# Scores of two pairs in one operation, five attention banks and three layer banks, and other assumed times in a planned kernel

## The chip, the cores and the metric

The kernel runs on one core of a Trainium2 chip. Five engines work side by side, each through its own instructions in order: PE (TensorE, the matrix products), DVE (VectorE), ACT (ScalarE), POOL (GpSimd) and SP (SyncE, which here issues every DMA). Matrix products write to PSUM, which has eight banks; DVE and ACT read them out to SBUF. The metric is the time of one execution on the device in microseconds, the median of several runs; less is better.

## The reference

Two attentions are computed from q, k, v of shape (8, 8, 576, 64) and added, and the sum goes through two dense layers with a maximum of three products:

```python
q_d, k_d, v_d = (a.reshape(B, H, S // 4, 4, D).mean(axis=3) for a in (q, k, v))
out_up = np.repeat(sm_attn(q_d, k_d, v_d), 4, axis=2)        # pooled attention
mask = np.abs(pos[:, None] - pos[None, :]) < 4               # seven neighbours
out_local = softmax(np.where(mask, scale * q @ k.T, -1e9)) @ v
x = (out_up + out_local).transpose(0, 2, 1, 3).reshape(4608, 512)
h = np.maximum(np.maximum(x @ w1, x @ w2), x @ w3)           # 512 -> 768
return h @ w_out                                             # 768 -> 512
```

All of it is float32. (The lines are shortened; `sm_attn` is a softmax attention with the scale 1/8.)

## The kernel before

**Tiling.** The 4608 tokens are cut into nine blocks of 512: block j < 8 is the first 512 tokens of batch j, and block 8 holds the last 64 tokens of all eight batches. The attention of a block has two groups, n = 2j and 2j+1, each of four heads in two pairs (`pr` = 0, 1); so the groups run from 0 to 17. The layers of a block (`mlp_in`, `mlp_out`) follow its attention.

**Layers.** Operands are split into a high and a low float32r part, and three products stand for one. `mlp_in(j)` has 6 x 3 accumulations of 12 matmuls of 128x512; ACT or DVE reads each bank out (into `t`, with the maximum), then ACT and DVE split the result into `hh`. `mlp_out(j)` has 4 accumulations of 18 matmuls, read by ACT into `y` and stored. That is 288 layer matmuls per block. Each layer bank is a tile of the tag `pm`.

**Attention.** For a group from 4 on: `load_qk` loads a q and k tile per pair (three buffers); `window_scores` computes a pair's scores against 70 neighbours for each 64 queries, 16 float32 products into two banks of the tag `pa` (a float32 product shows as two passes in the profile, 32 in all); `scores` copies them to `sm`, stores them to a scratch in DRAM with two DMAs per pair, and loads back the seven diagonals as `s` for the softmax. `values` multiplies and adds `v` on ACT, POOL and DVE. Beside it `pooled_scores` makes the pooled attention with three `pa` banks, stores the transposed probabilities to DRAM in eight DMAs (`pdd`) and loads them as `pt` (one DMA) and `ptt` (two); `pooled_values` multiplies them with the pooled v into one `pa` bank, read by ACT as `od`. Then `transposes` adds `od` to x and splits the sum into `xhi` and `xlo`. The groups 0 to 3 (`DENSE`) do the neighbours by a banded product instead (`band_scores`, `band_values`); block 0 takes its banks for that from `pm`, block 1 from `pa`.

**Order.** No instruction is issued when its line runs. A `Recorder` collects all operations, and `place` makes a list schedule of them on assumed costs: of the operations that are ready on an engine it takes the first, by priority, and an operation that opens a tile waits until its buffers are free. The buffers of a tag are given out in the order in which tiles were recorded. `emit` then issues everything in the planned order from line 415, which is why every row of the profile shows L415. On the chip each engine runs its own list in order; where an input is later than assumed, the engine waits and all behind it too.

PE operations of the attention have a priority 2000 ahead of their group's, so they go before layer matmuls as soon as the plan has them ready. The layers have priority -100, `transposes` -200, group n has 100n, and the weights have 60 to 350. `together()` makes several PE calls one operation that nothing else is put between, with 200 ns for the turn (`RUN_NS`).

Margins in the plan: `lag` (600 ns) is added between an operation and a user on another engine, `pelag` in its place where the user is on PE, `dlag` is the least that is added behind a DMA, and the costs of all engines but PE are multiplied by `SLOW`. The line that applies them:

```python
u.ready = max(u.ready, free[e] if same else o.end + max(u.lag, u.dlag if e == "SP" else 0.0))
```

A DMA is assumed to take 530 ns of SP (times the factor) and to land 1200 ns plus its bytes plus 1100 ns later. Layers, `transposes` and the groups 0 to 3 have neither `dlag` nor factor. The order of the `pa` banks around a group: three of `pooled_scores(n)`, two and two of the scores of group n+1 (`begin(n + 1)` is recorded there), one of `pooled_values(n)`, three of `pooled_scores(n + 1)`.

Of the kernel before, what the change touches and what calls it, by code (L numbers as in the profile page):

```python
# [10 lines left out]
F32 = mybir.dt.float32  # L11
# [5 lines left out]
PSUM = bass.MemoryType.PSUM  # L17
# [3 lines left out]
P = 128  # L21
NO = 7
FAC = 4
# [8 lines left out]
XBUFS = 5  # L32
VBUFS = 3
LAG = 600.0
PELAG = 2500.0
DMA_LAG = 2000.0
SLOW = 1.15
SEG = FAC * P
QT = 64
KWIN = QT + NO - 1  # L40
# [4 lines left out]
DENSE = tuple(range(2 * BANDED))  # L45
# [71 lines left out]
class Recorder:  # L117
# [6 lines left out]
    def __init__(self, nc, tc, sb, psum, dr):  # L124
        self.nc, self.tc, self.pools = nc, tc, {"SB": sb, "PSUM": psum, "DRAM": dr}
        self.names = bacc.Bacc("TRN2", target_bir_lowering=False, num_devices=1)
        self.ops, self.tags, self.of, self.masks = [], {}, {}, {}
        self.prio, self.lag, self.pelag, self.run = 0.0, 0.0, 0.0, None
        self.engines = {"PE": nc.tensor, "DVE": nc.vector, "ACT": nc.scalar, "POOL": nc.gpsimd, "SP": nc.sync}

    def tile(self, shape, dtype, tag=None, bufs=1, name=None, space="SB"):
# [32 lines left out]
    def add(self, forms, bias={}):  # L164

        o = Op()
        o.forms, o.bias = forms, bias
        outs, ins = [], []
        for method, args, kw in next(iter(forms.values())):
            named = [k for k in ("out", "accum_out") if is_ap(kw.get(k))]  # L170
            w = [kw[k] for k in named]
            r = [a for a in args if is_ap(a)] + [v for k, v in kw.items() if is_ap(v) and k not in named]
            if "out" not in named:
                w.append(args[0])
                r = r[1:]
            outs += w
            ins += r
        o.prio = self.prio
        if "PE" in forms and o.prio >= 0.0:
            o.prio -= 2000.0  # L180
        o.dlag = 0.0 if self.pelag == self.lag else DMA_LAG
        o.lag = self.lag if "PE" not in forms else self.pelag
        o.seq = len(self.ops)
        o.need, o.tiles = set(), []
        pe = "PE" in forms
        for write, aps in ((False, ins), (True, outs)):
            for ap in aps:
                r = self.region(ap)
                if r is None:
                    continue  # L190
                info, p0, p1, m = r
                bufs, order = self.tags[info["tag"]]
                assert info["k"] == 0 or info["k"] + bufs >= len(order), ("used after its buffer was given on", info["name"])
                for q, w, a0, a1, am, was_pe in info["acc"]:
                    if (w or write) and q is not o and (info["psum"] or (a0 < p1 and p0 < a1 and (am & m))) and not (w and write and info["tag"][0] == "DRAM"):
                        o.need.add(q)
                if not info["ops"] or info["ops"][-1] is not o:
                    info["ops"].append(o)
                    o.tiles.append(info)
                if write and info["psum"] and pe:  # L200
                    info["acc"] = [x for x in info["acc"] if not (x[1] and x[5])]
                info["acc"].append((o, write, p0, p1, m, pe))
        self.ops.append(o)
        return o
# [37 lines left out]
    def place(self):  # L242
        ops = self.ops
        for o in ops:
            o.users, o.left, o.ready, o.eng, o.waits = [], len(o.need), 0.0, None, []
            o.cost = {}
            for e, calls in o.forms.items():
                c = [self.price(e, *x) for x in calls]
                turn = RUN_NS if e == "PE" and len(calls) > 1 else 0.0
                o.cost[e] = ((sum(x[0] for x in c) + turn) * (1.0 if e == "PE" or not o.dlag else SLOW), any(x[1] for x in c))  # L250
        for o in ops:
            for q in o.need:
                q.users.append(o)
# [179 lines left out]
def local_global_attention_maxout_kernel(ctx: ExitStack, tc: tile.TileContext, qk_d, qke_d, vw_d, wi_d, wo_d, v, ident_d, mask_d, diag_d, band_d, out):  # L433
# [8 lines left out]
        return rec.tile(shape, dtype, tag, bufs, name)  # L442

    def bank(shape, tag, name):
        return rec.tile(shape, F32, tag, {"pm": 4, "pa": 4}[tag], name, "PSUM")

    @contextmanager
    def at(prio, lag=0.0, pelag=None):
        was = rec.prio, rec.lag, rec.pelag
        rec.prio, rec.lag, rec.pelag = prio, lag, lag if pelag is None else pelag  # L450
        yield
        rec.prio, rec.lag, rec.pelag = was

    @contextmanager
    def together():
# [34 lines left out]
    state = {}  # L490
# [183 lines left out]
        act.mul(odtail[:, c, j], po[:, :, P:], 0.25)  # L674


    def window_scores(n, pr, tag="pa"):
        step = QT if n // 2 < B else KWIN
        qk = state[n]["qk"][pr]
        sps = [bank([P, FAC, KWIN], tag, f"sb_{n}_{pr}_{i}") for i in range(2)]  # L680
        with together():
            for t in range(SEG // QT):
                u, h = divmod(t, 2)
                for i in range(2):
                    pp = slice(64 * i, 64 * i + 64)
                    pe.matmul(sps[i][QT * h : QT * h + QT, u], qk[pp, 0, 3 + QT * t : 3 + QT * t + QT], qk[pp, 1, step * t : step * t + KWIN], start=True, stop=True, tile_position=(64 * i, QT * h))
        return sps

    def scores(n):
        j = n // 2  # L690
        st = state[n]
        scr = rec.tile([SCR], F32, "scr", 2, f"scr_{n}", "DRAM")
        for pr in range(2):
            sps = window_scores(n, pr)
            sm = new([P, 2, FAC, KWIN], tag="sm", bufs=2, name=f"sm_{n}_{pr}")
            for i in range(2):
                copy(sm[:, i], sps[i])
            for h in range(2):
                to = (2 * pr * SEG + h * QT) * (KWIN + 1)
                sp.dma_start(dram(scr, to, [[KWIN, QT], [P * (KWIN + 1), 2 * FAC], [1, KWIN]]), sm[QT * h : QT * h + QT].rearrange("p g u x -> p (g u) x"))  # L700
        s = st["p"] = new([P, FAC, HH, NO], tag="s", bufs=2, name=f"s_{n}")
        sp.dma_start(s, dram(scr, 0, [[FAC * (KWIN + 1), P], [KWIN + 1, FAC], [SEG * (KWIN + 1), HH], [1, NO]]))
        e0 = 0 if j < B else FAC
        sf = s[..., e0 : e0 + 3]
        dve.tensor_tensor(out=sf, in0=sf, in1=mask[:, j // B].unsqueeze(2).broadcast_to([P, FAC, HH, 3]), op=ALU.min)
        mx = new([P, FAC, HH], tag="mx", bufs=2, name=f"mx_{n}")
        dve.tensor_reduce(out=mx, in_=s, axis=AX.X, op=ALU.max)
        dve.tensor_tensor(out=s, in0=s, in1=mx.unsqueeze(3).broadcast_to([P, FAC, HH, NO]), op=ALU.subtract)
        act.activation(s, s, AF.Exp, scale=0.125)
        z = new([P, FAC, HH], tag="z", bufs=2, name=f"z_{n}")  # L710
        dve.tensor_reduce(out=z, in_=s, axis=AX.X, op=ALU.add)
        dve.tensor_scalar_add(z, z, EPS)
        dve.reciprocal(z, z)
        dve.tensor_tensor(out=s, in0=s, in1=z.unsqueeze(3).broadcast_to([P, FAC, HH, NO]), op=ALU.mult)
# [42 lines left out]
            vw[g] = t  # L757

    def band_scores(n, pr, tag):
        sps = window_scores(n, pr, tag)  # L760
        sm = new([P, 2, FAC, KWIN], tag="sm", bufs=2, name=f"sm_{n}_{pr}")
        for i in range(2):
            dve.tensor_tensor(out=sm[:, i], in0=sps[i], in1=bandmask, op=ALU.min)
        mx = new([P, 2, FAC], tag="mxb", bufs=2, name=f"mxb_{n}_{pr}")
        z = new([P, 2, FAC], tag="zb", bufs=2, name=f"zb_{n}_{pr}")
        dve.tensor_reduce(out=mx, in_=sm, axis=AX.X, op=ALU.max)
        dve.tensor_scalar_mul(mx, mx, -0.125)
        for i in range(2):
            for u in range(FAC):
                act.activation(sm[:, i, u], sm[:, i, u], AF.Exp, bias=mx[:, i, u : u + 1], scale=0.125, accum_out=z[:, i, u : u + 1])  # L770
        dve.tensor_scalar_add(z, z, EPS)
        dve.reciprocal(z, z)
        muls = [("mul", (sm[:, i, u], sm[:, i, u], z[:, i, u : u + 1]), {}) for i in range(2) for u in range(FAC)]
        one = [("tensor_tensor", (), dict(out=sm, in0=sm, in1=z.unsqueeze(3).broadcast_to([P, 2, FAC, KWIN]), op=ALU.mult))]
        rec.add({"DVE": one, "POOL": one, "ACT": muls})
        state[n]["sm", pr] = sm
# [114 lines left out]
    def attention(n):  # L891
# [21 lines left out]
            tail_pooled(n)  # L913
            pooled_scores(n)
        if n < 2 * B + 1:
            with at(100.0 * n + 100.0, LAG, PELAG):
                begin(n + 1)
        values(n)
        if j < B:
# [1 line left out]

    def block(j):
        for n in (2 * j, 2 * j + 1):
            with at(100.0 * n, LAG, LAG if n in DENSE else PELAG):
                attention(n)
        if DENSE and 2 * j + 1 == DENSE[-1]:
            with at(100.0 * n + 100.0, LAG, PELAG):
                begin(n + 1)

    def turn(j):  # L930
# [49 lines left out]
```

## Time and profile before

| what | value |
|---|---|
| median of 3 runs | 736.38 us (734.8 to 737.51) |
| the profiled execution | 741.36 us, its span 739.5 us |
| DMA | 100.28 MB, mean 136 GB/s |
| DVE busy, 20 to 140 us | 111.8 of 120 us |

The profile is one execution. A busy PE row is not a rate: a 128x512 matmul shows 0.39 us but the next starts after 0.23, so starts are counted. In a row of the stretches stand the stretch, its length, then busy time and (in brackets) instructions of PE, PE's weight loads, DVE, ACT and POOL, then the granted clock of PE, the DMA share and GB/s. In a row of the timeline stand the start, the duration, the engine, the operation, the tile written and the tiles read, the shape, the count, and in square brackets the idle time before it and what ended that. In PE's list of waits stand the total, the count and the longest. Buffer numbers are left out of names, and a name such as `t` or `wo` is a buffer that several tiles share.

### The profile page before, as it was taken

Reading aid. Unit: us, or ns where it says so; the run is one execution under the profiler, and the core shown is the slowest. Engines: PE = TensorE matmul, PEld = TensorE weight load, DVE = VectorE, ACT = ScalarE, POOL = GpSimd, SP = SyncE. Lnnn points to the kernel's source line nnn. Section 1 sums busy time; section 2 is a strip of 40 time slices with the busy share of each in tenths; the row PEclk is TensorE's granted clock in tenths of the full one; section 3 lists DMA queues with packets and bytes.
Section 4 is the critical chain, followed back from the end, with each engine's and each line's share of the span. In section 5 each row is a group of like instructions: output and inputs, shape, how many; then the busy total and the mean of one; then the engine's idle time right before and its main releaser. Section 6 shows DMA issues by size and latency. Waiting matters only on the chain.

```text
span 739.5 us, 13101 instructions
## 1 busy us (share of the span) xinstructions
PE 698.1 (94%) x4544; PEld 559.7 (76%) x4544; DVE 523.3 (71%) x1002; ACT 396.3 (54%) x1359; POOL 175.0 (24%) x265
## 2 busy tenths in 40 slices
PE   3749999999999999999998999999989999999997
PEld 2637777778787787878686878787867888888885
DVE  6899999847978887878886869788775677331220
ACT  4685565447748284846656456477572675121111
POOL 0002000005524251543523133134151332000000
PEclk9959999999999999999999999999999999999999
DMA  8945321676585677847675746585866551120002
GB/s 285 364 133 194 119 98 58 184 169 148 134 175 143 160 163 177 182 97 149 175 151 148 160 126 136 160 161 139 151 189 120 104 150 34 26 71 29 1 0 58
DMA packets 189599, 100.28 MB, mean 136 GB/s; under 512 B 161262, under 2 KB 165389, under 8 KB 188765
## 3 DMA queue, kind: packets, MB, share of 16 engines
q1 hardware_dynamic: 189533, 99.44, 53.6%
q8 instruction: 36, 0.59, 0.3%
q14 instruction: 30, 0.25, 0.1%
HBM read 70.18 MB, written 29.23 MB: 134 GB/s over the span
## 4 chain that ended last, share of the span: by engine, by line
PE 72%; DVE 11%; DMA 10%; SPq 3%; issue 2%; ACT 2%; DVEq 0%; ACTq 0%
PE pm L415 65%; PE pa L415 6%; SPq L415 3%; DMA traw<-in_v_dram 3%; DVE pvb L415 2%; DMA qk<-in_qk_dram 2%; DVE wo L415 2%; DVE t L415 2%; DMA ptt<-pdd 1%; DVE sm L415 1%; DMA out_dram<-y 1%; DMA x<-in_vw_dram 1%; DMA pt<-pdd 1%; ACT pvb L415 1%; DMA pvb<-in_wo_dram 1%
## 5 line engine op out<-in xcount | busy, mean ns | idle before, releaser
L415 PE MATMUL pm<-xlo_0r,whi_0r 128*128 128x512 f32 x648 | 254.8, 393 | 0.0
L415 PE MATMUL pm<-xhi_0r,wlo_0r 128*128 128x512 f32 x648 | 253.8, 392 | 0.0
L415 PE MATMUL pm<-xhi_0r,whi_0r 128*128 128x512 f32 x648 | 253.4, 393 | 0.0
L415 POOL TENSOR_TENSOR pvb<-v,s 128x256 f32<-128x256 f32 x209 | 147.0, 734 | 192.8 <-DVE s L415 61.7
L415 ACT ACTIVATE pvb<-v,s 128x64 f32<-128x64 f32 x732 | 184.7, 340 | 9.7 <-DVE s L415 5.1
L415 DVE TENSOR_TENSOR t<-pm,t 128x512 f32<-128x512 f32 x108 | 74.2, 687 | 99.3 <-PE pm L415 95.3
L415 PEld LDWEIGHTS pm<-xhi_0r,whi_0r 128*128 128x128 f32 x648 | 121.9, 188 | 26.4 <-issue 1.1
L415 PEld LDWEIGHTS pm<-xlo_0r,whi_0r 128*128 128x128 f32 x648 | 121.8, 188 | 26.4 <-issue 0.9
L415 PEld LDWEIGHTS pm<-xhi_0r,wlo_0r 128*128 128x128 f32 x648 | 121.9, 188 | 25.6 <-issue 0.6
L415 DVE TENSOR_TENSOR pvb<-pvb 128x768 f32<-128x768 f32 x112 | 99.0, 884 | 10.9 <-POOL pvb L415 8.7
L415 ACT CAST hh_0r<-t 128x512 fp32r<-128x512 f32 x54 | 33.5, 621 | 133.9 <-DVE t L415 133.6
L415 PE MATMUL pm<-wo_1r,hh_0r 128*128 128x512 f32 x216 | 85.2, 395 | 0.0
L415 PE MATMUL pm<-wo_0r,hh_1r 128*128 128x512 f32 x216 | 84.8, 394 | 0.0
L415 PE MATMUL pm<-wo_0r,hh_0r 128*128 128x512 f32 x216 | 83.2, 393 | 1.4 <-ACT wo_0r L415 0.9
L415 ACT COPY t<-pm 128x512 f32<-128x512 f32 x54 | 31.6, 585 | 40.4 <-PE pm L415 40.3
L415 ACT COPY y<-pm 128x512 f32<-128x512 f32 (+1 forms) x44 | 25.4, 583 | 50.3 <-PE pm L415 40.9
L415 PEld LDWEIGHTS pm<-wo_0r,hh_0r 128*128 128x128 f32 x216 | 40.4, 188 | 10.9 <-ACT wo_0r L415 1.8
L415 PEld LDWEIGHTS pm<-wo_1r,hh_0r 128*128 128x128 f32 x216 | 40.6, 188 | 9.7 <-DVE wo_1r L415 0.8
L415 PEld LDWEIGHTS pm<-wo_0r,hh_1r 128*128 128x128 f32 x216 | 40.5, 188 | 8.7 <-issue 0.4
L415 DVE TENSOR_TENSOR hh_1r<-t,hh_0r 128x512 fp32r<-128x512 f32 x54 | 38.7, 717 | 9.9 <-ACT hh_0r L415 9.6
L415 ACT CAST xhi_0r<-t 128x512 fp32r<-128x512 f32 x32 | 19.5, 617 | 16.7 <-DVE t L415 12.6
L415 PEld LDWEIGHTS pa<-qk 64*64 64x64 f32 x1024 | 18.9, 133 | 12.1 <-issue 4.4
(119 smaller groups left out, 706.6 us busy)
## 6 DMA issues: line engine op xcount, KB each, us to landing
qk<-in_qk_dram SPq DMA_DIRECT2D x32, 582.0 KB
v<-in_v_dram SPq DMA_DIRECT2D x55, 320.0 KB
out_dram<-y SPq DMA_DIRECT2D x36, 256.0 KB
scr<-sm SPq DMA_DIRECT2D x56, 140.0 KB
xd<-x SPq DMA_DIRECT2D x112, 64.0 KB
t<-xd SPq DMA_DIRECT2D x28, 256.0 KB
wo<-in_wi_dram SPq DMA_DIRECT2D x4, 1536.0 KB
pdd<-pd SPq DMA_DIRECT2D x48, 80.0 KB
```

Source lines behind the costliest of these rows:

```text
L415: getattr(self.engines[o.eng], method)(*map(real, args), **{k: real(x) for k, x in kw.items()})
```

## The change

Four things at once.

- `window_scores` takes a list of pairs and puts the products of all of them into one `together()`. `scores` calls it for both pairs, so one PE operation opens four `pa` banks and makes 32 products; the copies and DMAs follow per pair as before. `band_scores` calls it with one pair.
- The PSUM banks are divided anew: `pa` has five instead of four, `pm` three instead of four.
- `PELAG`, `DMA_LAG` and `SLOW` give way to a triple by group: below group 8 `pelag` 2000, `dlag` 1500, factor 1.1; from group 8 on 3000, 3000, 1.2. Before, it was 2500, 2000, 1.15 for all groups from 4 on.
- Groups 0 to 3 have no triple (`None`): then `pelag` is `lag`, `dlag` 0 and the factor 1, as before.

```diff
-PELAG = 2500.0
-DMA_LAG = 2000.0
-SLOW = 1.15
+CARE = {"near": (2000.0, 1500.0, 1.1), "far": (3000.0, 3000.0, 1.2)}
+NEAR = 8
...
-        o.dlag = 0.0 if self.pelag == self.lag else DMA_LAG
-        o.lag = self.lag if "PE" not in forms else self.pelag
+        pelag, o.dlag, o.slow = self.care or (self.lag, 0.0, 1.0)
+        o.lag = pelag if "PE" in forms else self.lag
...
-                o.cost[e] = ((sum(x[0] for x in c) + turn) * (1.0 if e == "PE" or not o.dlag else SLOW), any(x[1] for x in c))
+                o.cost[e] = ((sum(x[0] for x in c) + turn) * (1.0 if e == "PE" else o.slow), any(x[1] for x in c))
...
-        return rec.tile(shape, F32, tag, {"pm": 4, "pa": 4}[tag], name, "PSUM")
+        return rec.tile(shape, F32, tag, {"pm": 3, "pa": 5}[tag], name, "PSUM")
...
+    def care(n):
+        return None if n in DENSE else CARE["near" if n < NEAR else "far"]
...
-    def window_scores(n, pr, tag="pa"):
+    def window_scores(n, prs, tag="pa"):
         step = QT if n // 2 < B else KWIN
-        qk = state[n]["qk"][pr]
-        sps = [bank([P, FAC, KWIN], tag, f"sb_{n}_{pr}_{i}") for i in range(2)]
+        sps = {pr: [bank([P, FAC, KWIN], tag, f"sb_{n}_{pr}_{i}") for i in range(2)] for pr in prs}
         with together():
-            for t in range(SEG // QT):
+            for pr in prs:
+                qk = state[n]["qk"][pr]
+                for t in range(SEG // QT):
...
+        both = window_scores(n, range(2))
         for pr in range(2):
-            sps = window_scores(n, pr)
+            sps = both[pr]
...
-            with at(100.0 * n + 100.0, LAG, PELAG):
+            with at(100.0 * n + 100.0, LAG, care(n + 1)):
                 begin(n + 1)
...
-            with at(100.0 * n, LAG, LAG if n in DENSE else PELAG):
+            with at(100.0 * n, LAG, care(n)):
                 attention(n)
```

More of the change, by code (lines that the diff above doesn't have):

```diff
@@ L127, in __init__ @@
         self.ops, self.tags, self.of, self.masks = [], {}, {}, {}
-        self.prio, self.lag, self.pelag, self.run = 0.0, 0.0, 0.0, None
+        self.prio, self.lag, self.care, self.run = 0.0, 0.0, None, None
         self.engines = {"PE": nc.tensor, "DVE": nc.vector, "ACT": nc.scalar, "POOL": nc.gpsimd, "SP": nc.sync}
@@ L444, in bank, with at @@
     def bank(shape, tag, name):
-        return rec.tile(shape, F32, tag, {"pm": 4, "pa": 4}[tag], name, "PSUM")
+        return rec.tile(shape, F32, tag, {"pm": 3, "pa": 5}[tag], name, "PSUM")
     @contextmanager
-    def at(prio, lag=0.0, pelag=None):
-        was = rec.prio, rec.lag, rec.pelag
-        rec.prio, rec.lag, rec.pelag = prio, lag, lag if pelag is None else pelag
+    def at(prio, lag=0.0, care=None):
+        was = rec.prio, rec.lag, rec.care
+        rec.prio, rec.lag, rec.care = prio, lag, care
         yield
-        rec.prio, rec.lag, rec.pelag = was
+        rec.prio, rec.lag, rec.care = was
+    def care(n):
+        return None if n in DENSE else CARE["near" if n < NEAR else "far"]
     @contextmanager
@@ L674, in pooled_values @@
         act.mul(odtail[:, c, j], po[:, :, P:], 0.25)
-    def window_scores(n, pr, tag="pa"):
+    def window_scores(n, prs, tag="pa"):
         step = QT if n // 2 < B else KWIN
-        qk = state[n]["qk"][pr]
-        sps = [bank([P, FAC, KWIN], tag, f"sb_{n}_{pr}_{i}") for i in range(2)]
+        sps = {pr: [bank([P, FAC, KWIN], tag, f"sb_{n}_{pr}_{i}") for i in range(2)] for pr in prs}
         with together():
-            for t in range(SEG // QT):
[L683 to L686, printed above, removed]
+            for pr in prs:
+                qk = state[n]["qk"][pr]
+                for t in range(SEG // QT):
+                    u, h = divmod(t, 2)
+                    for i in range(2):
+                        pp = slice(64 * i, 64 * i + 64)
+                        pe.matmul(sps[pr][i][QT * h : QT * h + QT, u], qk[pp, 0, 3 + QT * t : 3 + QT * t + QT], qk[pp, 1, step * t : step * t + KWIN], start=True, stop=True, tile_position=(64 * i, QT * h))
         return sps
@@ L759, in band_scores @@
     def band_scores(n, pr, tag):
-        sps = window_scores(n, pr, tag)
+        sps = window_scores(n, (pr,), tag)[pr]
         sm = new([P, 2, FAC, KWIN], tag="sm", bufs=2, name=f"sm_{n}_{pr}")
@@ L923, in block @@
         for n in (2 * j, 2 * j + 1):
-            with at(100.0 * n, LAG, LAG if n in DENSE else PELAG):
+            with at(100.0 * n, LAG, care(n)):
                 attention(n)
         if DENSE and 2 * j + 1 == DENSE[-1]:
-            with at(100.0 * n + 100.0, LAG, PELAG):
+            with at(100.0 * n + 100.0, LAG, care(n + 1)):
                 begin(n + 1)
```

## The prediction

> **What bounds the kernel now.** I read the page's busy rows and slices first, then busy time by stretch, the groups of matmuls, the chain of waits and PE's own list of waits.
>
> ```profile
> span 739.5 us, 13101 instructions
> PE 698.1 (94%) x4544; PEld 559.7 (76%) x4544; DVE 523.3 (71%) x1002; ACT 396.3 (54%) x1359; POOL 175.0 (24%) x265
> PE   3749999999999999999998999999989999999997
> PEclk9959999999999999999999999999999999999999
> ```
>
> PE is busy from the fourth slice to the last, at full clock but for the third slice. The stretches price a layer matmul, and the groups count them:
>
> ```profile
> 55.00:149.00 94.00, 92.24 (x771) 71.36 (x771) 86.59 (x157) 52.41 (x155) 7.45 (x11) 1.00 0.42 132
> ...
> 603.00:717.00 114.00, 114.00 (x505) 94.48 (x504) 39.62 (x61) 31.56 (x84) 10.03 (x15) 1.00 0.13 34
> ```
>
> ```profile
> L415 PE MATMUL pm<-xhi_0r,whi_0r 128*128 128x512 f32 x648 | 253.4, 393 | 0.0
> ...
> L415 PE MATMUL pm<-wo_0r,hh_0r 128*128 128x512 f32 x216 | 83.2, 393 | 1.4 <-ACT wo_0r L415 0.9 <-ACT hh_0r L415 0.5
> ```
>
> From 603 to 717 us 505 layer matmuls start in 114.00 us, with nothing between them: 0.226 us each. There are three groups of 648 and three of 216, 2592 in all, so 585 us of the span is layer work that the change leaves as it is. The first of them starts here:
>
> ```profile
> 54.66 0.69 PE L415 MATMUL pm<-xhi_0r,whi_0r 128*128 128x512 f32 x1
> ```
>
> 54.7 + 585 is 639.4 us. The other 100 us is attention on PE, the turns between the two kinds of work, PE's stalls and the last store. The chain of waits ends in 158 us of layer work alone:
>
> ```profile
> 576.03 158.01 PE pm L415 x696
> ```
>
> So the attention is finished that long before the end, and from 55 us on only what PE itself spends or waits counts. A change there is worth its PE time; before 55 us, DVE and the loads count.
>
> **Part 1: two score operations become one.** A pair's scores are a run of 32 passes between layer matmuls:
>
> ```profile
> 194.13 0.39 PE L415 MATMUL pm<-xhi_0r,whi_0r 128*128 128x512 f32 x1
> 194.45 0.72 PE L415 MATMUL pa<-qk 64*64 64x70 f32 x32
> 195.09 0.51 PE L415 MATMUL pm<-xlo_0r,whi_0r 128*128 128x512 f32 x1
> 195.43 0.40 PE L415 MATMUL pm<-xhi_0r,wlo_0r 128*128 128x512 f32 x1
> ```
>
> From 194.13 to 195.43 is 1.30 us and holds two layer steps, 0.45 us; the run costs 0.85 us. Its passes take 195.09 - 194.45 = 0.64 us, so entering and leaving cost 0.21 us. The merged run is 64 passes and one turn, so each of the 14 groups 4 to 17 saves one turn: **-2.9 us**. Groups 2 and 3 still go pair by pair. No instruction is added; the copies and the four stores to the scratch follow as before. The added wait: all four banks must be free before the first pass, and behind it on PE stand the layer matmuls. With five banks, two are free beside the three of the pooled scores, so two of those must have been read by ACT's exponentials, where today's second pair needs all three. PE's list of waits (below) has no wait on a qk load, so the second pair's load hides as it does now; uncovered, it would cost its landing.
>
> **Part 2: assumed times.** These move no instruction's own cost, only its place in the order. PE's waits after 140 us:
>
> ```profile
> PE pa L415 <- DMA pt<-pdd: 3.2, 3, 1.8
> PE pa L415 <- DMA ptt<-pdd: 2.0, 2, 1.8
> PE pa L415 <- ACT pd L415: 0.8, 1, 0.8
> PE pa L415 <- ACT pdt L415: 0.6, 1, 0.6
> PE pm L415 <- ACT hh_0r L415: 0.5, 1, 0.5
> ```
>
> 5.2 us is waiting for the pooled probabilities to come back from DRAM. The largest case beside a clean one, in PE's timeline:
>
> ```profile
> 389.88 0.39 PE L415 MATMUL pm<-xlo_0r,whi_0r 128*128 128x512 f32 x1
> 390.79 0.47 PE L415 MATMUL pa<-pt,vd 128*64 128x144 f32 x4 [0.52 <-DMA pt<-pdd]
> 393.09 0.75 PE L415 MATMUL pa<-ptt,vtail 128*64 128x144 f32 x4 [1.83 <-DMA ptt<-pdd]
> ...
> 394.73 1.33 PE L415 MATMUL pa<-qkT 64*128 64x144 f32 x8
> ...
> 396.55 0.50 PE L415 MATMUL pm<-xhi_0r,wlo_0r 128*128 128x512 f32 x1
> ...
> 434.69 0.39 PE L415 MATMUL pm<-wo_0r,hh_0r 128*128 128x512 f32 x1
> ...
> 437.20 0.50 PE L415 MATMUL pm<-wo_1r,hh_0r 128*128 128x512 f32 x1
> ```
>
> The same work takes 396.55 - 389.88 = 6.67 us at group 10 and 437.20 - 434.69 = 2.51 us at group 11. Of the 4.2 us excess 2.35 is idle; the other 1.8 is slow matmuls, since the clock drops:
>
> ```profile
> 380.00:400.00 20.00, 17.65 (x89) 13.68 (x88) 12.01 (x28) 6.76 (x24) 7.25 (x13) 0.91 0.67 169
> ```
>
> 9% of 20 us is the same 1.8 us. The Trainium skill ("TensorE: Matmul & The Clock Gate", "What's actually happening") says that the clock falls to half after about one idle window of 3.4 us that runs freely; the trace agrees in the drop, though 2.35 us idle was enough here. By it a shorter stall would lose the slow matmuls whole, and the sum would stay as it is below.
>
> The other waits of late groups:
>
> ```profile
> 538.64 0.47 PE L415 MATMUL pa<-pt,vd 128*64 128x144 f32 x4 [1.78 <-DMA pt<-pdd]
> 539.26 0.47 PE L415 MATMUL pa<-ptt,vtail 128*64 128x144 f32 x4 [0.15 <-DMA ptt<-pdd]
> ...
> 572.41 0.47 PE L415 MATMUL pa<-pt,vd 128*64 128x144 f32 x4 [0.91 <-DMA pt<-pdd]
> ```
>
> Group 14 idles 1.9 us, with 1.8 us of slow matmuls as at group 10, 3.7; group 15 0.9; a score run waiting for ACT 0.8. With 4.2 that makes 9.6 us. For groups from 8 on the plan adds 3000 - 2500 = 500 ns before PE may use a landed load, 3000 - 2000 = 1000 ns between the stores and that load, and 1.2 for 1.15 on each cost. An SP issue is then assumed at 530 x 1.2 = 636 ns, was 610; the row says 650:
>
> ```profile
> L415 SPq DMA_DIRECT2D ptt<-pdd x24: 610/650/692, 166.7 to 567.8; - x24
> ```
>
> Eleven issues make 0.3 us, so PE's turn comes about 1.8 us later. Taken from idle times of 2.35, 1.93, 0.91 and 0.8 that leaves 0.6 us, so up to 9.0 us is recovered; nothing, if later turns are met by equally later loads. I take two thirds, **-6.0 us**, since three of eight late groups waited and the two big ones are cured by the delay alone. PE has layer matmuls to fill it; nothing is late next, with 158 us in hand.
>
> Groups 4 to 7 get 500 ns less at each of the two hops and 1.1 for 1.15. The plan assumes about 2.4 us of landing (1200 + 1100 ns and the bytes); with 2.0 us of margin that is 4.4 us. Two late loads took:
>
> ```profile
> 387.90 5.15 DMA ptt<-pdd
> ...
> 534.95 4.18 DMA ptt<-pdd
> ```
>
> By the one an early group would wait 0.75 us, by the other nothing. For groups 5, 6, 7 that is 0 to 2.3 us; **+0.5 us**, nearer nothing, because none of them waits today.
>
> **Part 3: one layer bank less.** An accumulation is 12 matmuls (2.7 us) in a layer's first half, 18 (4.1 us) in its second. In the steady state the bank given up costs nothing while ACT or DVE reads a bank within two accumulations, 5.4 us. It counts where PE runs ahead into several banks because an input is late. Two such places, with the input that comes last and the pm matmuls issued before it:
>
> ```profile
> 221.00:233.90 12.90, 9.62 (x40) 1.00 0.60 168
> 120.80:143.40 22.60, 14.80 (x54) 1.00 0.53 157
> ```
>
> ```profile
> 233.23 0.68 DVE L415 TENSOR_TENSOR xlo_0r<-t,xhi_0r 128x512 fp32r<-128x512 f32 x1
> ...
> 142.79 0.65 ACT L415 CAST wo_0r<-pvb 128x512 fp32r<-128x512 f32 x1 [0.46 <-DVE pvb L415]
> ```
>
> At the start of layer 2 the fourth xlo is there at 233.9. Three banks hold 3 x 11 = 33 matmuls that do without it; 40 were issued, so 7 x 0.226 = 1.6 us has no bank. In layer 0's second half the last output weight is there at 143.4; three banks hold 3 x 15 = 45, 54 were issued: 2.0 us. Below, the plan fills both with other work (0); above, the whole bank, 2.7 and 4.1 us. I take **+3.6 us**, the count of the rows.
>
> The start has it too: block 0's band work uses the layer banks.
>
> ```profile
> 25.74 1.21 PE L415 MATMUL pm<-qk 64*64 64x70 f32 x32
> ...
> 31.23 0.69 DVE L415 TENSOR_TENSOR t<-pm,od 128x512 f32<-128x512 f32 x1 [0.81 <-ACT od L415]
> ```
>
> ```profile
> 35.67 0.73 DVE L415 TENSOR_REDUCE mxb<-sm 128x8 f32<-128x560 f32 x1
> ```
>
> Group 1's first scores at 25.74 take two banks while two value banks wait to be read from 31.23 on. With three they must wait till 31.9, six us later, but the first reduction is at 35.67, so most of it hides; DVE's copies move. Bounds -1 (five attention banks loosen block 1) and +3 (half of the six); I take **+0.5**.
>
> **Sum:** -2.9 - 6.0 + 0.5 + 3.6 + 0.5 = -4.3 us on the profiled 741.36 us (span 739.5 and 1.9 around it), 737.1. The median shown, 736.38, lies 5.0 lower; the same difference gives **732.1 us**, 0.6% faster.
>
> **The rivals.** What a measurement can tell from no change is 0.5%, 3.7 us: below 732.7 and above 740.1.
>
> *The late stalls move, they don't go.* The loads follow ACT, DVE and SP, all replanned. For it: five of the eight late groups met their loads without a wait under the old margin, so lateness depends on the order. Against: the two large waits are short of the added 1.8 us by 0.6 at most. Without part 2's gain: -2.9 + 0.5 + 3.6 + 0.5 = +1.7, **738.1 us**.
>
> *Three banks starve the layers: slower.* Place: the first accumulations of layers 1 to 3 and layer 0's second half, where x or weights come just in time. Price: a bank's worth each, 3 x 2.7 + 4.1 = 12.2 us, with half of part 2: -2.9 - 3.0 + 0.5 + 12.2 + 0.5 = +7.3, **743.7 us**. For it: 55 to 149 us has DVE busy for 86.59 of 94 us, so a late reader can't catch up. Against: from 603 to 717 us no bank waits at all. It decides once bank waits exceed 2.9 + 6.0 + 3.7 - 1.0 = 11.6 us.
>
> *Bank waits that also drop the clock.* Each could cost the 1.8 us of the 0.91 row; once in each of nine layers is 16.2 us, -4.3 + 16.2 = +11.9, **748.3 us**. The slices show no drop with four banks except beside DMA stalls. The Trainium skill (the same page, "A second HAM failure mode: psum-queue depth-cycling") tells of such a kernel, whose PE idled between groups as it cycled through banks; no run here shows it yet.
>
> *Everything lands:* -2.9 - 9.0 and nothing given back, -11.9, **724.5 us**.
>
> **Chances.** The forecast 0.48, everything landing 0.08; the moved stalls 0.24; starved banks 0.17, with the clock 0.03. The forecast's own range (728 to 736) lies partly inside 0.5%: I leave 0.42 of its 0.48 on the faster side, so faster 0.50, same 0.30, slower 0.20. Range 724.5 to 742: it leaves out the clock case, half of the starved banks and the best end of "everything".
>
> **What would show it.** Score runs of x64 with one turn (about 1.5 us between layer matmuls), 14 of them. PE's waits on pt and ptt near 1 us instead of 5.2, and a granted clock of 1.00 from 60 us on. PE waiting for ACT t, DVE t or ACT y ahead of pm matmuls near 120 to 150 and 220 to 235 us would be the bank's price. The first layer matmul at 54 to 58 us. The forecast is wrong if layer 0's second half ends more than 4 us later than before, or if pt waits return at other groups.

## The result and the profile after

| | before | changed |
|---|---|---|
| median | 736.4 us (734.8 to 737.51, 6 runs) | 729.13 us (727.95 to 733.91, 6 runs) |
| ratio, 95% | | 0.9915 (0.9886 to 0.9944) |
| profiled execution, its span | 741.36, 739.5 us | 728.81, 726.4 us |
| first layer matmul | 54.66 us | 55.51 us |

The ratio takes 0.85% off, 6.3 us, and the medians lie 7.3 us apart; 4.3 us were forecast. The page of the changed kernel begins as follows (span, busy time of each engine, then two rows in 40 slices):

```profile
span 726.4 us, 13076 instructions
PE 688.0 (95%) x4544; PEld 555.2 (76%) x4544; DVE 520.1 (72%) x993; ACT 399.4 (55%) x1365; POOL 177.1 (24%) x268
PE   2739999999999999999999999999999999999996
PEclk9959999999999999999999999999999999999999
```

The two 8s that PE's row had in its second half are 9s now, and PE has as many matmuls as before. The stretches of the changed kernel (columns as before, the granted clock third from the end) say the same from 60 us on, the last row being pure layer work:

```profile
60.00:380.00 320.00, 317.20 (x2236) 253.76 (x2237) 262.37 (x511) 196.33 (x683) 88.50 (x133) 1.00 0.62 152
380.00:580.00 200.00, 199.48 (x1324) 161.26 (x1323) 150.68 (x288) 115.14 (x412) 65.94 (x97) 1.00 0.65 145
603.00:717.00 114.00, 114.00 (x505) 94.39 (x504) 43.71 (x68) 34.96 (x101) 11.43 (x17) 1.00 0.17 41
```

In its last 200 us of attention PE lacks 0.5 us, and the 505 layer matmuls still start in 114.00 us. PE's list of waits of the changed kernel, 140 to 720 us, is complete here:

```profile
PE pa L414 <- DMA ptt<-pdd: 0.6, 1, 0.6
PE pm L414 <- DVE hh_1r L414: 0.5, 1, 0.5
PE pm L414 <- DVE xlo_0r L414: 0.4, 1, 0.4
PE pm L414 <- ACT hh_0r L414: 0.2, 1, 0.2
```

The 5.2 us of waiting for `pt` and `ptt` are 0.6. In PE's timeline of the changed kernel, here are a score run with its neighbours and group 10's pooled values, which took 6.67 us before:

```profile
187.31 0.39 PE L414 MATMUL pm<-xhi_0r,wlo_0r 128*128 128x512 f32 x1
187.62 1.21 PE L414 MATMUL pa<-qk 64*64 64x70 f32 x64
188.76 0.50 PE L414 MATMUL pm<-xhi_0r,whi_0r 128*128 128x512 f32 x1
189.10 0.40 PE L414 MATMUL pm<-xlo_0r,whi_0r 128*128 128x512 f32 x1
...
392.14 0.39 PE L414 MATMUL pm<-xhi_0r,whi_0r 128*128 128x512 f32 x1
392.46 0.47 PE L414 MATMUL pa<-pt,vd 128*64 128x144 f32 x4
...
394.65 0.50 PE L414 MATMUL pm<-xlo_0r,whi_0r 128*128 128x512 f32 x1
```

From 187.31 to 189.10 is 1.79 us with two layer steps, 0.45 us, in it: the merged run costs 1.34 us where two runs cost 2 x 0.85. That is 0.36 us less a group, and there are 14 such runs in the trace, the first at 133.71 and the last at 577.60. Group 10's passage takes 394.65 - 392.14 = 2.51 us, as a clean one.

**A measure that leaves the start out.** Each layer has 288 layer matmuls, so the 289th begins layer 1 and the 2017th layer 7. In the changed kernel they are these two rows of PE's timeline:

```profile
150.42 0.40 PE L414 MATMUL pm<-xhi_0r,whi_0r 128*128 128x512 f32 x1
...
590.24 0.39 PE L414 MATMUL pm<-xhi_0r,whi_0r 128*128 128x512 f32 x1
```

From one to the other is 439.82 us. This stretch holds all attention groups but the first few. The table has it for every kernel that was profiled, beside the sum of PE's list of waits from 155 to 600 us and the time lost to a granted clock under 1 (that of each 10 us from 155 to 605, its lack times 10 us, added up). The kernels after the second row are told in the next section; each row is one execution.

| kernel | layer 1 starts | 1 to 7 | waits | lost to clock |
|---|---|---|---|---|
| before, first profile | 148.88 | 454.43 | 6.5 | 3.4 |
| changed | 150.42 | 439.82 | 1.7 | 0 |
| e1 before again | 150.00 | 447.60 | 3.3 | 0 |
| e2 merge only | 148.12 | 461.35 | 13.7 | 8.5 |
| e3 times only | 147.74 | 451.60 | 4.9 | 1.7 |
| e4 banks only | 154.33 | 442.07 | 0.2 | 0 |
| e5 merge and banks | 148.52 | 447.64 | 8.0 | 0 |
| e6 banks and times | 153.66 | 442.04 | 0.6 | 0 |
| e7 late groups old | 153.93 | 449.99 | 8.0 | 1.7 |
| e8 early groups old | 149.15 | 439.69 | 2.6 | 0 |
| e9 three and four banks | 155.60 | 446.87 | 3.8 | 0 |
| e10 late margins alone | 154.66 | 442.17 | 3.6 | 0 |
| e11 late factor alone | 150.03 | 451.54 | 8.8 | 1.7 |
| e12 all groups late | 156.50 | 445.75 | 5.7 | 3.5 |

Where "1 to 7" is long, PE waits or runs at a lower clock. With the last two columns taken off, 437 to 441 us are left in the kernels with merged scores and 441 to 445 in the others. The measure has a spread of its own: the kernel before, whose PE order is the same in both rows, has 454.43 and 447.60. So a difference of a few us between two rows is a sign, and the ratios of the next section decide.

### The profile page after: what moved, and what is told of

It is laid out like the page before. It is cut to its first block, busy times and chain, and to the rows that moved or that the text cites. A ratio compares the mean times of both kernels' runs of the same rounds, so it can differ in the third digit from the quotient of the medians.

```text
span 726.4 us, 13076 instructions
## 1 busy us (share of the span) xinstructions
PE 688.0 (95%) x4544; PEld 555.2 (76%) x4544; DVE 520.1 (72%) x993; ACT 399.4 (55%) x1365; POOL 177.1 (24%) x268
## 4 chain that ended last, share of the span: by engine, by line
PE 59%; DVE 2%; DMA 2%; SPq 1%; POOL 0%; issue 0%; ACT 0%; DVEq 0%; ACTq 0%
PE pm L414 55%; PE pa L414 4%; SPq L414 1%; DMA t<-xd 1%; DVE pvb L414 1%; DMA pdd<-pd 0%; DMA ptt<-pdd 0%; POOL pvb L414 0%; DVE t L414 0%; DVE hh_1r L414 0%; DVE x L414 0%; DVE pd L414 0%; DVE xlo_0r L414 0%; ACT y L414 0%; DVE sm L414 0%
## 5 line engine op out<-in xcount | busy, mean ns | idle before, releaser
L414 ACT ACTIVATE pvb<-v,s 128x64 f32<-128x64 f32 x728 | 182.0, 339 | 12.3 <-DVE s L414 7.7
L414 DVE TENSOR_TENSOR pvb<-pvb 128x768 f32<-128x768 f32 x112 | 100.5, 897 | 8.0 <-ACT pvb L414 3.8
L414 POOL TENSOR_TENSOR hv<-v 128x128 f32<-128x128 f32 (+1 forms) x19 | 14.1, 745 | 74.5 <-DMA v<-in_v_dram 55.7
```

What stands on the lines that cost most here:

```text
L414: getattr(self.engines[o.eng], method)(*map(real, args), **{k: real(x) for k, x in kw.items()})
```

## The experiments

All kernels compute everything. e1 to e4 ran beside the kernel before at 735.88 us, e5 to e8 beside 736.3, e9 to e12 beside 734.9 (medians of 23, 35 and 27 runs). Two experiments of different calls are compared by their ratios to it.

**e1, the kernel before once more.** No edit.

> The kernel before, unchanged, profiled once more. If the two long waits of PE for the pooled probabilities (groups 10 and 14 in the first profile, 4.2 and 3.7 us with their slow matmuls) belong to the planned order, they return at the same two groups, and the profiled time lies near 741 us. If they are an accident of that one execution, other groups wait, or none does, and the profiled time lies near the median of 736 us.

Measured: 735.57 us, span 733.8. In its timeline, the pooled values of groups 10 and 14:

```profile
390.69 0.47 PE L415 MATMUL pa<-pt,vd 128*64 128x144 f32 x4 [0.31 <-DMA pt<-pdd]
391.31 0.47 PE L415 MATMUL pa<-ptt,vtail 128*64 128x144 f32 x4 [0.15 <-DMA ptt<-pdd]
...
534.72 0.47 PE L415 MATMUL pa<-pt,vd 128*64 128x144 f32 x4 [1.36 <-DVE s L415]
```

The same groups are late, but by 0.46 us where the first profile had 2.35, and by 1.36 where it had 1.93; the row of the second names DVE's `s` and not the load. All of its waits for `pt` and `ptt` after 155 us are 0.9 us, where the first profile had 5.2. No clock falls behind them. Its stretch 1 to 7 is 6.8 us shorter; waits and clock together are 6.6 us less. So most of the stalls of the first profile, which was 5 us above the median, are missing in this execution, which lies near it.

**e2, the merge alone.** In the changed kernel:

```diff
-CARE = {"near": (2000.0, 1500.0, 1.1), "far": (3000.0, 3000.0, 1.2)}
+CARE = {"near": (2500.0, 2000.0, 1.15), "far": (2500.0, 2000.0, 1.15)}
...
-        return rec.tile(shape, F32, tag, {"pm": 3, "pa": 5}[tag], name, "PSUM")
+        return rec.tile(shape, F32, tag, {"pm": 4, "pa": 4}[tag], name, "PSUM")
```

> Only the merged scores; four banks each, old assumed times. Theory A (turns): a merged run costs 1.34 us and two single ones 1.70 us, so 14 x 0.36 = 5.0 us less, 731.4 us, whatever the order. Theory B (banks): the merged run needs all four attention banks at once, so it comes later and the pooled work behind it too; then less than 2 us are gained, 734.5 us or more.

Measured: 748.4 us (745.97 to 749.35), ratio 1.0159 (1.0133 to 1.0186). Of its list of waits from 155 to 600 us two rows, then a stretch, then from its timeline a group's pooled scores and the next group's scores:

```profile
PE pm L414 <- ACT xhi_0r L414: 4.8, 3, 1.8
...
PE pm L414 <- DVE xlo_0r L414: 2.4, 2, 1.4
...
```

```profile
225.00:235.00 10.00, 6.06 (x32) 4.09 (x32) 6.79 (x9) 9.41 (x37) 8.65 (x11) 0.58 0.53 158
```

```profile
229.63 1.33 PE L414 MATMUL pa<-qkT 64*128 64x144 f32 x8
...
244.58 1.20 PE L414 MATMUL pa<-qk 64*64 64x70 f32 x64
```

7.2 us of the waiting is at layer matmuls for `xhi` and `xlo`, the result of the attention, and near 230 us the clock falls behind it. With four `pa` banks the merged operation must have all of them free: it starts 14.95 us behind the pooled scores here, the longest of 12 such gaps (the shortest is 7.0; in the kernel before they go from 6.0 to 9.9). The layers' input comes late with it. A saving of 5 us in PE time turns into a loss.

**e3, the new times alone.** The changed kernel with the pairs apart and the banks as before:

```diff
-        both = window_scores(n, range(2))
...
-            sps = both[pr]
+            sps = window_scores(n, (pr,))[pr]
...
-        return rec.tile(shape, F32, tag, {"pm": 3, "pa": 5}[tag], name, "PSUM")
+        return rec.tile(shape, F32, tag, {"pm": 4, "pa": 4}[tag], name, "PSUM")
```

> Only the new assumed times; two runs per group, four banks each. Theory A: the waits for pooled probabilities of groups 8 to 15 fall to below 1 us in the profile, and the time falls by 3 to 6 us, 730.5 to 733.5 us. Theory B (the order only changes by chance): waits return at other groups, within 2 us of before.

Measured: 738.0 us (734.32 to 740.53), ratio 1.0029 (1.001 to 1.0049). Of its list of waits from 155 to 600 us, the first three rows:

```profile
PE pm L414 <- ACT hh_0r L414: 2.5, 2, 1.7
PE pm L414 <- DVE xlo_0r L414: 1.4, 1, 1.4
PE pa L414 <- DMA ptt<-pdd: 0.4, 1, 0.4
...
```

The waits for `pt` and `ptt` are gone as they should, all but 0.4 us (of e1's 0.9). Others stand in their place, at layer matmuls for `hh` and `xlo`. That is the rival "the late stalls move, they don't go".

**e4, the banks alone.** In the kernel before:

```diff
-        return rec.tile(shape, F32, tag, {"pm": 4, "pa": 4}[tag], name, "PSUM")
+        return rec.tile(shape, F32, tag, {"pm": 3, "pa": 5}[tag], name, "PSUM")
```

> Only the banks, five for attention and three for the layers. Theory A: PE finds no bank where it ran ahead of its inputs (second half of layer 0, start of layer 2), 1.6 + 2.0 us, so 2 to 4 us more, 738.5 to 740.5 us. Theory B: the plan fills those places with other work and the fifth attention bank loosens block 1; within 1 us of before or faster.

Measured: 730.73 us (729.81 to 735.24), ratio 0.9944 (0.9922 to 0.9965), 4.1 us faster by the ratio, where the prediction has +4.1 us for this part. (The profiled execution took 734.78 us, 4 us over the median; ahead of layer 1 a score run waits 2.68 us for `sm` in it, and the clock is 0.72 from 146 to 152 us, 1.7 us lost.) Between 155 and 600 us PE waits once, 0.2 us. The timelines show what differs; first the kernel before, from a group's pooled scores (`qkT`) to the next group's first score run; then the same place of e4:

```profile
251.59 0.76 PE L415 MATMUL pa<-qkT 64*128 64x144 f32 x8
...
261.04 0.72 PE L415 MATMUL pa<-qk 64*64 64x70 f32 x32
```

```profile
253.62 0.76 PE L415 MATMUL pa<-qkT 64*128 64x144 f32 x8
...
254.69 0.72 PE L415 MATMUL pa<-qk 64*64 64x70 f32 x32
...
257.40 0.72 PE L415 MATMUL pa<-qk 64*64 64x70 f32 x32
```

The pooled scores hold three `pa` banks. With four, one is left and a pair needs two, so the next scores come 9.45 us later, after ACT has read. With five, the first pair follows at once, 1.07 us behind, and the second at 3.78. It is so at all 12 such places of the two traces: the first scores come 1.1 to 2.9 us behind in e4, 6.0 to 9.9 in the kernel before. The load of `pt` is issued earlier too, 24.7 us behind the pooled scores (the median of the 12 groups) instead of 28.1, and no load is late for PE. The last group's pooled values run at 557.36 us without a wait, where they waited until 572.41 before.

That the earlier loads are due to the scores is read from these gaps; no run moved the scores alone, and e9 below, with four banks and late scores, has 25.4 us. Nor is it what makes the change fast. There the merge needs four banks, and the gap is as long as it was or longer, 6.5 to 12.4 us at the 12 places (the changed kernel's timeline):

```profile
248.66 0.76 PE L414 MATMUL pa<-qkT 64*128 64x144 f32 x8
...
259.23 1.20 PE L414 MATMUL pa<-qk 64*64 64x70 f32 x64
```

**e5, merge and banks, old times.** The first line of e2's edit alone, on the changed kernel.

> The change with the old assumed times (2500, 2000, 1.15 for all groups from 4 on). Theory A (banks and turns): the fifth attention bank gives about 5 us as it did alone, and the merged runs 14 x 0.36 = 5 us on top, so about 726 us, no slower than the whole change. Theory B (the times are needed): merged runs move the pooled loads, so waits for pt and ptt return without the longer times, 732 us or more.

Measured: 736.55 us (732.33 to 744.1), ratio 1.0012 (0.9986 to 1.0037). Of its list of waits from 155 to 600 us:

```profile
PE pa L414 <- DMA pt<-pdd: 2.2, 2, 1.7
PE pm L414 <- DVE hh_1r L414: 2.1, 2, 1.7
...
PE pa L414 <- DMA ptt<-pdd: 1.1, 1, 1.1
...
```

On top of e4 the merge loses 0.68%, 5.0 us, though it saves as much in turns. 8.0 us of waits come in, for `pt` and `ptt` among them. The merged scores again come late: at the place that e4's rows show, the one run of 64 starts 6.72 us behind the pooled scores, since it needs four banks and five less three leaves two (e5's timeline):

```profile
256.80 0.76 PE L414 MATMUL pa<-qkT 64*128 64x144 f32 x8
...
263.52 1.20 PE L414 MATMUL pa<-qk 64*64 64x70 f32 x64
```

Late scores alone don't decide it, though. e8 below differs from e5 by the late groups' longer times only; its gaps are about as long (6.7 to 12.8 us, e5's 6.0 to 14.1), it has no wait for `pt` or `ptt` from 155 us on, and its ratio is 0.8% lower. So what costs is late scores with margins that are too short for them.

**e6, banks and times, pairs apart.** The first three lines of e3's edit alone.

> The change without the merging. Theory A: as the banks alone, 730 to 733 us, since the banks alone already left no wait for pt or ptt. Theory B: the times help only with the banks; then 726 to 728 us, and the merging is worth little.

Measured: 731.5 us (730.22 to 739.13), ratio 0.9954 (0.993 to 0.9979). The same as e4 within both intervals, and 1 to 7 is 442.04 against 442.07 us: without the merge the new times are worth nothing that these runs can show.

**e7 and e8, the change with one side's times old.**

```diff
-CARE = {"near": (2000.0, 1500.0, 1.1), "far": (3000.0, 3000.0, 1.2)}
+CARE = {"near": (2000.0, 1500.0, 1.1), "far": (2500.0, 2000.0, 1.15)}
```

That is e7; e8 has the old triple at "near" in its place.

> The change, but the groups from 8 on keep the old assumed times (2500, 2000, 1.15); the early groups keep the shorter ones. If the longer times of the late groups are what spares PE its waits, pt and ptt waits come back at groups 8 to 15, 2 to 4 us more than the change, 731 to 733 us. If not, within 1 us of the change, 728 to 730 us.

> The change, but the groups 4 to 7 keep the old assumed times; the late groups have the longer ones. In the profile of the change PE waits 0.6 us on ptt at group 7: with the old margin that goes, so up to 1 us less, 728 to 729 us, by theory A. If the shorter times are needed to have x in time for the layers 2 and 3, PE waits for xhi or xlo there and the time is 2 us or more above the change.

Measured: e7 740.95 us (733.96 to 749.4), ratio 1.0054 (1.0025 to 1.0083); e8 729.18 us (728.21 to 737.5), ratio 0.9932 (0.9907 to 0.9958). The longer times of the late groups are worth the difference between e7 and the change, 1.4%, or that between e5 and e8, 0.8% (each ± 0.4); the 2 to 4 us that were expected of e7 were too few. In the eight late groups 5.5 to 16.7 us lie between the issue of the `pt` load and its first use in the change, 4.3 to 11.3 in e7, and in e7's timeline group 8 waits again:

```profile
325.47 0.47 PE L414 MATMUL pa<-pt,vd 128*64 128x144 f32 x4 [2.85 <-DMA pt<-pdd]
```

The shorter times of groups 4 to 7 make no difference: 729.18 against 729.13.

**e9, three and four banks.** The kernel before with `{"pm": 3, "pa": 4}` and the eighth bank unused, to price the layers' bank without the fifth of attention.

> The kernel before with three layer banks and still four attention banks; one bank of PSUM is unused. It prices the layer bank alone. Theory A (the fifth attention bank is what gains, the layer bank costs a little, hidden in the sum of the banks experiment, which was 5 us faster): 1 to 4 us above before, 737 to 740 us, with PE later in layer 0's second half. Theory B (three layer banks make a better order by themselves): faster than before by 2 us or more.

Measured: 740.37 us (739.17 to 741.25, five runs), ratio 1.0072 (1.0047 to 1.0097), +5.3 us. The price is where the prediction put the larger of its two places, at the output weights of layer 0's second half (e9's timeline):

```profile
146.67 0.98 PE L415 MATMUL pm<-wo_0r,hh_0r 128*128 128x512 f32 x3 [2.32 <-ACT wo_0r L415]
...
148.19 0.50 PE L415 MATMUL pm<-wo_1r,hh_0r 128*128 128x512 f32 x1 [0.54 <-DVE wo_1r L415]
```

2.9 us of waiting for `wo`, against 0.9 and 1.1 in the two profiles of before. From layer 1 on nothing is lost that can be seen: 1 to 7 is 446.87 us, e1's 447.60. What the rest of the 5.3 us is stays open; the clock may have a part. This execution has half of it from 57 to 61 us, where the changed kernel has all (e1 has half too). Over the whole span the mean granted clock on record is 0.978 or 0.979 in four of the five runs (0.996 in the fifth), and 0.985 in the middle of the 27 runs of the kernel before beside them. That would be 0.0065 of 738 us, 4.8 us at most, an estimate. But the four of the 27 with 0.979 or less took 734.13 to 739.33 us, no more than the others. The stretch:

```profile
57.00:61.00 4.00, 4.00 (x42) 3.22 (x44) 2.67 (x4) 0.82 (x1) 3.02 (x2) 0.50 0.29 85
```

**e10, e11 and e12, which part of the long times works, and where.** The triple "far" is (3000, 3000, 1.15) in e10 and (2500, 2000, 1.2) in e11; e12 has `NEAR = 0`, so the long triple holds for groups 4 to 7 too.

> The change with the late groups' margins (3000, 3000) but the old factor 1.15 on costs. With the old margins and the old factor 741 us, with the whole change 729 us. If the margins behind DMAs and ahead of PE are what keeps the merged order from waiting, 729 to 732 us and no wait on pt or ptt over 1 us. If the factor does it, 736 us or more with those waits.

> The change with the late groups' factor 1.2 but the old margins (2500, 2000). If the margins do it, 736 us or more, with waits on pt or ptt at late groups. If the factor does it, 729 to 732 us.

> The change with the longer times for all groups from 4 on. If only the late groups need them, and early ones lose nothing by them since the two settings tried so far for groups 4 to 7 gave the same 729 us, 728 to 731 us. If x for layers 2 and 3 comes too late by it, PE waits on xhi or xlo at the start of these layers and it is 2 us or more above the change.

Measured: e10 731.77 us (729.93 to 739.87), ratio 0.9974 (0.9946 to 1.0002); e11 739.95 us (737.46 to 744.91), ratio 1.0066 (1.0034 to 1.0097); e12 736.61 us (734.6 to 740.44), ratio 1.0021 (0.9998 to 1.0043). The two margins do most of it, and the factor alone does nothing: e11 keeps e7's waits (its row for `pt`, 155 to 600 us, first below) and its time. Whether the factor adds to the margins is open. e10 is 0.59% (± 0.40) above the change, but five of its twelve runs, 734.87 us and more, have 0.975 to 0.980 of the clock on record; the other seven lie from 729.93 to 732.05 us. e12 has no wait for `pt` or `ptt` at all; its timeline (second) has a layer starving in their place, near 528 us and not at layers 2 or 3, where it was expected:

```profile
PE pa L414 <- DMA pt<-pdd: 5.1, 4, 2.4
```

```profile
527.61 1.11 PE L414 MATMUL pm<-xhi_0r,whi_0r 128*128 128x512 f32 x3 [2.78 <-ACT xhi_0r L414]
```

So margins that are long from group 4 on bring the attention too late for layer 6 in this execution, the slowest of e12's twelve, and those of the change, long from group 8 on, do not. Of the 12.0 us that its span is above the changed kernel's, 6.1 lie ahead of layer 1. No kernel here clearly beats the change; e8 equals it.

**The ladder.** From these ratios, in per cent of the kernel before:

| step | ratio | step is worth | in 1 to 7 |
|---|---|---|---|
| one layer bank less (e9) | 1.0072 | +0.72% (+5.3 us) | -0.7 us from e1 |
| a fifth bank for attention (e4) | 0.9944 | -1.28% (-9.4 us) | -4.8 us |
| the merge on top (e5) | 1.0012 | +0.68% (+5.0 us) | +5.6 us |
| the new times on top (the change) | 0.9915 | -0.97% (-7.1 us) | -7.8 us |

The half-widths of two ratios, added as squares, make each step below the first uncertain by 0.3 to 0.4%. The first two steps share the doubt of e9's clock: up to 4.8 us of the one and of the other may be that. The column on the right compares single executions. In the other order, times before merge, the steps from e4 are +0.1% (e6) and -0.39% (the change, ± 0.38). The change against e4 is -0.29% ± 0.36: what the merge and the new times together add to the new banks isn't clear of the noise. Two signs speak for a small gain, 1 to 7 (2.2 us less) and where the runs mostly lie (five of the change's six from 727.95 to 730.11 us, eight of e4's twelve from 729.81 to 732.20). Merge and new times with four banks each were not run, so that the change needs the fifth attention bank is not shown.

## Why the prediction was right, and where it was not

The sign is right and 729.13 us lies in the range, 3 us under the forecast. But its sum came out near by luck: two wrong terms, a gain for the times and a loss for the banks, stood against each other. (54.7 + 585 is 639.7, not 639.4; nothing hangs on it.)

- **Turns, -2.9 us: right in kind, too small.** The term's 0.21 us is measured as 0.36, so 14 groups save 5.0 us of PE's time. The passes of the old run were taken from its first start to the next matmul's, 0.64 us for 32. But 32 passes more make the run only 1.34 - 0.85 = 0.49 us longer, so 0.15 of the 0.64 belonged to the turn.
- **What the merge needs: the bank count was right, the price of waiting was missed.** The prediction said that with five banks only two of the pooled scores' three must have been read, and put nothing in the sum for it. e5 shows 8.0 us of new waits at that very setting with the old margins: the scores come 6.7 us behind the pooled scores at the place shown, where they come 1.1 behind in e4, and loads and layers are late. With four banks (e2) the merge is a loss of 1.59%, 11.7 us. The 158 us in hand at the end of the span are no cover: the layers need each group's result in turn, which e2's waits for `xhi` show.
- **Times of the late groups, -6.0 us: this step failed.** It took two thirds of the waits of one profiled execution as time to be had. Of that profile's 9.9 us of waits and lost clock the second profile has 3.3 (e1), and alone the new times take nothing off (e3, +2.1 us): the waits move, as the first rival has it. In the change the new times are worth 7.1 us (e5 against the change) to 10 (e7), but for waits that the merge makes, not those that the prediction counted. That 0.5 and 1.0 us of margin do most of it and the factor alone nothing (e10, e11) fits its reckoning, where the margins gave 1.5 of the 1.8 us.
- **Early groups, +0.5 us: nothing that can be measured** (e8).
- **One layer bank less, +3.6 us, and the start, +0.5:** layer 0's second half was put at 2.0 us; e9 waits 1.8 to 2.0 us longer for `wo` there. Layer 2's start was put at 1.6; there nothing was lost, 1 to 7 being no longer than in e1 and free of waits for `xhi` and `xlo`. The total of +5.3 (3.5 to 7.1) takes in the forecast 4.1, with the doubt about the clock, which leaves the bank itself 0.5 us at the least.
- **The fifth attention bank: the term that was missing.** It stood in the prediction only as a bound of -1 us at the start and as a condition for the merge. Without the merge it is worth -4.8 us between e9 and e4 in the stretch from layer 1 to 7, and -9.4 by the ratios, of which up to 4.8 may be e9's clock. The prediction never asked which operation of the kernel before was already held up by four banks, though the gap of 9.45 us between pooled scores and the next scores stood in its trace. What the bank is worth beside the merge no run shows.
- **Signs named in advance.** 14 runs of 64 passes, 1.34 us (about 1.5 was said); no wait for `t` or `y` in the two stretches that were to show the layer bank's price; `pt` and `ptt` waits 0.6 us (near 1); clock 1.00 from 60 us on; first layer matmul at 55.51 us (54 to 58): all as said. Layer 0's second half ends 1.5 us later than in the first profile, under the 4 us given as a limit.

The account of the merge in the last form can be closed to 1 us in 1 to 7, against e6, which differs by the merge alone: the 12 merged runs from 187.62 to 577.60 us save 12 x 0.36 = 4.3 us, waits grow by 1.1; -3.2 us by that, -2.2 measured.

**What stays open.** Why the merged order waits for its loads only at late groups under the old margins was not tried. A guess: the plan prices a layer matmul higher than the chip's step, so that PE comes earlier and earlier against the plan; nothing here tests it. What the fifth bank gives beside the merge, and what the factor adds to the margins, is open as said. Of e5's 5.6 us over e4, waits less turns explain 7.8 - 4.3 = 3.5.

## What to carry to other kernels

Before a bank (or any buffer) is taken from one user and given to another, look in the trace for the operation that already waits for one in the planned order: such a gap is no wait on the engine, because other work fills it, and it can still decide whether loads are late. It need not: e4 closed the gap, the change left it open and moved PE's use of the loads back, and both lost their waits. An operation that opens more buffers at once saves turns and pays with the time at which the last of them comes free; try it together with the buffers and the margins, not alone. And price stalls from two profiled executions or more, not from one that lies 5 us above the median.

## What the chip showed that was not expected

**The clock rises at different times in executions of one order.** The changed kernel and e10 issue the same PE work in the same order until about 283 us. In the timeline and the stretches of the changed kernel, then of e10:

```profile
57.02 1.15 PE L414 MATMUL pm<-y,x 70*64 70x64 f32 x30
59.89 1.20 PE L414 MATMUL pa<-qk 64*64 64x70 f32 x64
```

```profile
57.00:61.00 4.00, 4.00 (x113) 3.30 (x112) 4.00 (x5) 1.60 (x3) 1.36 (x2) 1.00 0.34 99
```

```profile
56.92 1.97 PE L414 MATMUL pm<-y,x 70*64 70x64 f32 x30
...
62.10 2.15 PE L414 MATMUL pa<-qk 64*64 64x70 f32 x64
```

```profile
57.00:61.00 4.00, 4.00 (x41) 3.23 (x43) 2.77 (x4) 0.92 (x1) 3.02 (x2) 0.50 0.26 81
61.00:70.00 9.00, 9.00 (x105) 7.04 (x102) 7.20 (x15) 4.08 (x17) 0.73 (x1) 0.81 0.66 229
```

The same 30 passes take 1.15 and 1.97 us, the same 64 take 1.20 and 2.15. PE of e10 runs at half pace for at least 5 us longer, and layer 1 starts at 154.66 us where it is 150.42. e7 and e11 share that order up to there too: e7, late like e10 (its rows are below), starts layer 1 at 153.93, e11, with 94 matmuls from 57 to 61 us, at 150.03. With such a difference by chance, a single profile can't tell changes of 4 us at the start, and the time from layer 1 to layer 7 is the better measure, within its own spread. The Trainium skill ("TensorE: Matmul & The Clock Gate", "What's actually happening") says that the clock's window runs freely, so that the moment of the rise varies from run to run, by 500 ns either way; the traces agree in kind, but the two moments lie at least 5 us apart here.

**The record of the clock can be missing.** e7's PE goes at e10's half pace here, and its stretch says 1.00 (timeline, then stretch, of e7):

```profile
61.81 2.15 PE L414 MATMUL pa<-qk 64*64 64x70 f32 x64
```

```profile
57.00:61.00 4.00, 4.00 (x44) 3.22 (x42) 2.49 (x4) 0.64 (x1) 3.03 (x2) 1.00 0.35 94
```

44 matmuls start in 4 us where the changed kernel starts 113. The Trainium skill (the same page, "Seeing it yourself") warns that these records are not to be trusted alone, and the trace agrees. The time of one known run of passes is the surer clock.
